# Order of the side work around a fused attention and MLP kernel: early differences, an earlier mean, and the weight differences one slot sooner

## The chip, the cores and the metric

The kernel runs on one core of a Trainium2 chip. The time is device microseconds of one execution, from runs on the chip; the median of the runs is given. A profiled execution gives, beside its time, when each instruction of each engine ran.

## The reference

Eight batches of eight heads, 576 tokens, head size 64; model width 512, hidden width 2048.

```python
scores = 1/sqrt(64) * q @ k.T                      # per batch and head
thresh = max(scores, -1) - tau
scores = where(scores >= thresh, scores, -1e9)
attn = exp(scores - max(scores, -1))
attn = attn / (sum(attn, -1) + 1e-09)
x = (attn @ v), heads side by side                 # (8, 576, 512)
mu, var = mean(x, -1), mean((x - mu)**2, -1)
xn = (x - mu) / sqrt(var + 1e-06) * g_ln
out = x + maximum(xn @ w_ch1, 0) @ w_ch2
```

w_ch1 is 512x2048 and w_ch2 2048x512. All products are done in float32.

## The kernel before, in words

**Slots.** The attention goes through 72 slots, nine for each batch. A slot takes 256 queries of each head of a pair (the fifth slot of a batch takes the last 64 queries of all heads). In a slot TensorE makes the scores (L394); VectorE reduces them to the negative maximum (L408); GpSimd makes the thresholds (L412); ScalarE takes the exponentials (L418); VectorE masks and sums them (L426) and takes the reciprocal (L431); GpSimd divides in four instructions (L442); VectorE transposes in blocks (L508); a DMA writes the result to a scratch tensor and another fetches it in the next slot (`fetch`, L519), and TensorE multiplies by v (L554), which ScalarE copies into `x` (L571). In slots whose successor needs a new pair of heads, `turn` (L331) scales q on GpSimd (L342) and transposes q and k on VectorE (L345 to L355).

**Groups.** The MLP goes through 16 groups of 288 tokens, two per batch. For each, GpSimd adds up x over its four pieces (`sum`, L586), TensorE turns that into a mean over all partitions (`mean_of`, L595, L601), ScalarE copies it out (L603), and VectorE subtracts it (`centre`, L606, L613: xc). `first_part` (L757) makes the hidden layer, and `second_quarters` (L903), or `second_plain` (L887) for group 0, makes the result.

**Seven products.** From group 1 on, six of the sixteen hidden tiles of the first part, and the whole second part, are done as a block product of two by two blocks with seven quarter products instead of eight. That needs sums and differences of blocks of both factors. Those of the tokens are made for each group: `xt3`, `xt2`, `xt4` on GpSimd (L752, L749, L752, in `quarters`, L835) and `xt1` on VectorE (L752). Those of the weights are made once, by the generator `differences` (L703): for w_ch1 (L715 to L719) s3 and s4 on GpSimd, s1 (in place) and s2 on VectorE, for two halves; for w_ch2 the same in 16 steps, four of each kind (L732). s1 overwrites what s3 reads; s2 reads s1; s4 reads s2. It is advanced by `first_part` of group 1, three steps after each tile (L874).

**Order.** All engines follow an order written out by hand. The loop over slots (L1081) calls the attention's steps, and at four quarters of a slot `second_part` (L1028), which takes steps of the MLP's generators as the plan `owed` has room. The MLP's additions and subtractions are put into lists, `rush` and `drops`, by `later` (L735), and `drip` (L622) empties these at the end of a slot's quarter by what room an engine has. An entry may be urgent: `drip` runs everything up to the last urgent entry that is due. `root` (L671, three instructions on VectorE, L674 to L678, which make the reciprocal square root of the variance more exact) is put into `rush` as urgent, due two quarters later if the norm is issued in the last quarter of a slot (L783). `need` (L744) runs a list until an entry is done.

**PSUM.** The MLP's products, the mean and the variance share two banks (`ps_ff`). While `second_quarters` runs, `banks_taken` keeps the mean out of them; the mean of the next group waits in `waiting_mean` and is issued within the last segment (L982 to L987).

The steps that the change touches are `differences`, `quarters`, the loop over tiles in `first_part` (L874), `second_plain`, and L983.

Of the kernel before, what the change touches and what calls it, by code (L numbers as in the profile page):

```python
# [12 lines left out]
ALU = mybir.AluOpType  # L13
# [5 lines left out]
def kernel(  # L19
# [31 lines left out]
    nc = tc.nc  # L51
# [5 lines left out]
    NK = DM // 128  # L57
# [5 lines left out]
    SLOTS = 2 * HP + 1  # L63
# [5 lines left out]
    SETS = [(5, 6, 7)]  # L69
# [58 lines left out]
    def load_v(u):  # L128
# [18 lines left out]
        out=tau_sb, in_=bass.AP(tensor=tau.tensor, offset=tau.offset, ap=[[0, 128], [1, 1]])  # L147
# [5 lines left out]
    for t in [er_sb] + v_rest:  # L153
# [10 lines left out]
        out=scl_sb, in0=tau_sb, scalar1=0.0, scalar2=SCALE, op0=ALU.is_ge, op1=ALU.mult  # L164
    )
    nc.vector.tensor_scalar(
        out=low_sb, in0=tau_sb, scalar1=0.0, scalar2=BIG, op0=ALU.is_lt, op1=ALU.mult
    )
    nc.vector.scalar_tensor_tensor(
        out=low_sb, in0=tau_sb, scalar=-1.0, in1=low_sb, op0=ALU.mult, op1=ALU.subtract  # L170
# [449 lines left out]
    aside, stores, drops, rush = [], [], [], []  # L620
# [50 lines left out]
    def root(y, x, t):  # L671
# [14 lines left out]
    w1 = {  # L686
        (i, j, k): w1_sb[NK // 2 * j + k][:, HD * 128 * i : HD * 128 * (i + 1)]
        for i in range(2)
        for j in range(2)
        for k in range(NK // 2)  # L690
    }
    w1_more = [
        [[t[:, k] for k in range(NK // 2)] for t in (
            consts.tile([128, NK // 2, len(ms) * 128], F32, name=f"w1_{q}_{ms[0]}") for q in (2, 3, 4)
        )]
        for ms in SETS
    ]
    more = []

    def part_tile(name):  # L700
        return ffn.tile([128, PART], F32, tag="part", bufs=2, name=name)

    def differences():  # L703


        flat = conversion.stage.rearrange("p a b -> p (a b)")
        flat4 = e_room[1].rearrange("p a b -> p (a b)")
        size = HM * HD * 128
        for t in (flat[:, :size], flat[:, size : 2 * size], flat4[:, :size]):
            more.append(t.rearrange("p (m d c) -> p m d c", m=HM, d=HD))  # L710
        for ms, (s2, s3, s4) in zip(SETS, w1_more):
            of = lambda i, j, k: w1[i, j, k][:, ms[0] * 128 : (ms[-1] + 1) * 128]
            for k in range(NK // 2):
                s1 = of(1, 0, k)
                nc.gpsimd.tensor_tensor(out=s3[k], in0=of(0, 0, k), in1=s1, op=ALU.subtract)  # L715
                yield
                nc.vector.tensor_tensor(out=s1, in0=s1, in1=of(1, 1, k), op=ALU.add)
                nc.vector.tensor_tensor(out=s2[k], in0=s1, in1=of(0, 0, k), op=ALU.subtract)
                nc.gpsimd.tensor_tensor(out=s4[k], in0=of(0, 1, k), in1=s2[k], op=ALU.subtract)  # L719
                yield  # L720
        s2, s3, s4 = more
        s1 = w2[1, 0]
        for eng, out, a, b, op in (
            (nc.gpsimd, s3, w2[0, 0], w2[1, 0], ALU.subtract),
            (nc.vector, s1, w2[1, 0], w2[1, 1], ALU.add),
            (nc.vector, s2, s1, w2[0, 0], ALU.subtract),
            (nc.gpsimd, s4, w2[0, 1], s2, ALU.subtract),
        ):
            for m in range(HM):
                for d in range(0, HD, 4):  # L730
                    at = (slice(None), m, slice(d, d + 4))
                    eng.tensor_tensor(out=out[at], in0=a[at], in1=b[at], op=op)  # L732
                    yield

    def later(calls_of, done, *calls, urgent=None, age=0):  # L735
        for what, cost, fn, eng, *args in calls:

            def go(what=what, fn=fn, eng=eng, args=args):
                fn(eng, *args)
                done.add(what)  # L740

            calls_of.append((urgent, now + age, eng, cost, go))

    def need(calls, done, *what):  # L744
        while not done.issuperset(what):
            calls.pop(0)[-1]()

    def add(eng, out, a, b):
        eng.tensor_tensor(out=out, in0=a, in1=b, op=ALU.add)  # L749

    def less(eng, out, a, b):
        eng.tensor_tensor(out=out, in0=a, in1=b, op=ALU.subtract)  # L752
# [4 lines left out]
    def first_part(g, done):  # L757
# [3 lines left out]
        plain = g == 0  # L761
# [3 lines left out]
        sums_of = differences() if g == 1 else iter(())  # L765
# [24 lines left out]
        def tile_of(d):  # L790
            p1 = ps_ff.tile([128, TOK], F32, tag="ff", name="p1")
            for c in range(NK):
                product(
                    p1, lhsT=w1_sb[c][:, d * 128 : (d + 1) * 128], rhs=xc[:, c],
                    start=(c == 0), stop=(c == NK - 1),
                )
                if c < NK - 1:
                    yield 1, 1
            nc.scalar.activation(hidden[:, d], p1, func=AF.Relu)  # L799
            yield 2, 1  # L800

        pool, dve = nc.gpsimd, nc.vector
        half = NK // 2
        ms = SETS[0]
# [3 lines left out]
        b11, b12 = xc[:, :half, early], xc[:, :half, late]  # L808
        b21, b22 = xc[:, half:, early], xc[:, half:, late]
        t2, t3 = hidden[:, ND - 3 : ND - 1, early], hidden[:, ND - 3 : ND - 1, late]  # L810
        t4, t1 = hidden[:, ND - 1].rearrange("p (c t) -> p c t", c=half), t3
        s2, s3, s4 = w1_more[0]
# [20 lines left out]
            yield 2, 0.5  # L833

        def quarters():  # L835
            later(
                rush, done, ("xt3", 1, less, pool, t3, b22, b12), ("xt2", 1, add, pool, t2, b11, t3),
                ("xt4", 1, less, pool, t4, b21, t2), urgent=pool,
            )
            yield quarter(1, old(0, 0), b11, h11)  # L840
            yield quarter(2, old(0, 1), b21)
            need(rush, done, "xt4")
            yield quarter(7, s3, t3)
            later(rush, done, ("xt1", 1, less, dve, t1, b12, b11), urgent=dve)
            yield quarter(6, s2, t2, h12)
            later(
                rush, done, ("xu2", 1, add, dve, h12, h12, h11), ("xu3", 1, add, dve, parts[7], parts[7], h12),
                ("x11", 1, add, pool, h11, h11, parts[2]), ("r11", 1, positive, pool, h11),
            )
            need(rush, done, "xt1")  # L850
            yield quarter(4, old(1, 1), t4, h21)
            later(rush, done, ("x21", 1, add, dve, h21, h21, parts[7]), ("r21", 1, positive, dve, h21))
            need(rush, done, "x11")
            yield quarter(3, s4, b22)
            later(rush, done, ("x12", 1, add, dve, h12, h12, parts[3]))
            yield quarter(5, old(1, 0), t1, h22)
            later(
                rush, done, ("xu4", 1, add, dve, h12, h12, h22), ("r12", 1, positive, dve, h12),
                ("x22", 1, add, dve, h22, h22, parts[7]), ("r22", 1, positive, dve, h22),
                urgent=dve,  # L860
            )
# [4 lines left out]
        for d in singles:  # L866
            while conversion.ended < 4 * (d // 4 + 1):
                yield 0, 0
            if d == low:
                yield from norm(True)  # L870
            if d == low + 2:
                need(rush, done, "root")
            yield from tile_of(d)
            for _ in range(1 if plain else 3):  # L874
                next(sums_of, None)
            ended += 1
            yield from norm()
            if not plain and d > 1:
                yield from next(between, ())
                yield from norm()  # L880
# [5 lines left out]

    def second_plain(g, rb, done):  # L887
        y = ffn.tile([128, NK, TOK], F32, tag="sq", bufs=1, name="y")
        for m in range(NK):
            p2 = ps_ff.tile([128, TOK], F32, tag="ff", name="p2")  # L890
            for d in range(ND):
                while conversion.ended <= conversion.n1 + 4 * m + d // 4:
                    yield 0, 0
                product(
                    p2, lhsT=w2_sb[:, m, d], rhs=hidden[:, d],
                    start=(d == 0), stop=(d == ND - 1),
                )
                if d < ND - 1:
                    yield 2, 1
            aside.append(lambda m=m, p2=p2: add_to_x(g, m, y[:, m], p2, rb))  # L900
            yield 2, 1

    def second_quarters(g, rb, done):  # L903

# [3 lines left out]
        s2, s3, s4 = more  # L908
        b11, b12 = hidden[:, :HD, early], hidden[:, :HD, late]
        b21, b22 = hidden[:, HD:, early], hidden[:, HD:, late]  # L910
# [39 lines left out]
        dve, pool = nc.vector, nc.gpsimd  # L950
# [29 lines left out]
        )  # L980
        yield 2, 0.5
        last = segment(s4, b22)  # L982
        for _ in range(12):  # L983
            yield next(last)
        banks_taken[0] = False
        while waiting_mean:
# [14 lines left out]
    QUARTERS = 4  # L1001
# [65 lines left out]
    else:  # L1067
# [3 lines left out]
        for i in range(ND):  # L1071
            nc.sync.dma_start(
                out=w2_sb[:, :, i],
# [123 lines left out]
```

## Time and profile before

| | |
|---|---|
| time, median of 3 runs | 1409.44 us (1409.41 to 1409.78) |
| the profiled execution: its own time | 1409.68 us |
| its span, first to last instruction | 1407.8 us |
| TensorE clock granted, mean | 0.991 |
| busy: TensorE, VectorE, GpSimd, ScalarE | 1327.4, 1024.6, 721.5, 497.2 us |
| TensorE busy, 0 to 190 us | 152.2 us |
| TensorE busy, 190 to 260 us (group 1's first part) | 59.84 us |
| TensorE busy, 260 to 1320 us | 1040.76 us |
| TensorE busy, 1320 to 1408 us | 74.55 us |
| slots 10, 11, 12 begin (scores on TensorE) | 193.03, 213.70, 234.18 us |

In the profile PE is TensorE, PEld its loading of weights, DVE VectorE, ACT ScalarE, POOL GpSimd and SP the engine that issues DMAs. A line number is that of the kernel's text. In a line of the order of time the columns are start and duration in us, engine, line, operation, the tile written and those read, shape and count of records; in brackets stands how long the engine was idle before, and whose instruction ended that. A matmul instruction shows as two records. L104 is a helper through which all products but the scores and the values go, so the tiles' names tell them apart: `p` is a tile of the first part, `quarter` and `seg` are quarter products of the first and the second part, `sc` scores or values. L749 and L752 are the helpers for additions and subtractions.

### The profile page before, as it was taken

The page shows a single profiled execution, that of the slowest core. Times are in us where ns is not written, and L with a number is a line of the kernel's source. Part 1 is how long each engine was busy: PE and PEld are TensorE (multiplying, and loading weights), DVE is VectorE, ACT ScalarE, POOL GpSimd, SP SyncE. Part 2 cuts the span into 40 slices and gives each one's busy share as a digit, 9 for nine tenths or more (in the row PEclk, how much of TensorE's full clock was granted, in tenths as well). Part 3 has the DMA queues.
Part 4 walks back from the last instruction along what each step waited for, and adds up shares of the span by engine and source line. Part 5 has one row for each costly group of instructions (what it writes and reads, how often), then busy time and mean ns, then how long its engine had stood idle before and what let it go on. Part 6 is the DMA issues. An engine that isn't in the chain of part 4 may idle for free. (4 is left out here: it accounts for less than half of the span.)

```text
span 1407.8 us, 38072 instructions
## 1 busy us (share of the span) xinstructions
PE 1327.4 (94%) x16128; PEld 1040.7 (74%) x16128; DVE 1024.6 (73%) x1680; ACT 497.2 (35%) x985; POOL 721.5 (51%) x887
## 2 busy tenths in 40 slices
PE   4878998999999999999999999999999999999996
PEld 3655665767878687876879677786978677786876
DVE  5997868767777788867777788767887777777331
ACT  3877623233232323323242323333242323323120
POOL 2444447554465555555455555555554544645433
PEclk8999999999999999999999999999999999999998
DMA  9612345346754466445755376455755376444211
GB/s 231 171 61 84 90 114 169 127 145 180 195 159 145 151 176 178 139 171 140 205 164 170 109 195 174 133 170 147 195 165 170 102 190 182 145 145 144 77 18 18
DMA packets 316393, 205.64 MB, mean 146 GB/s; under 512 B 242368, under 2 KB 273856, under 8 KB 308160
## 3 DMA queue, kind: packets, MB, share of 16 engines
q1 hardware_dynamic: 311456, 202.62, 50.2%
q8 instruction: 127, 2.08, 0.6%
q10 hardware_dynamic: 4736, 0.59, 0.4%
q14 instruction: 42, 0.34, 0.1%
q0 software_dynamic: 32, 0.00, 0.0%
HBM read 119.41 MB, written 83.76 MB: 144 GB/s over the span
## 5 line engine op out<-in xcount | busy, mean ns | idle before, releaser
L104 PE MATMUL p<-xc,w 128*64 128x288 f32 x2656 | 352.1, 409 | 24.0 <-ACT hidden L799 16.3
L408 DVE TENSOR_REDUCE neg<-sc 128x2 f32<-128x1152 f32 x144 | 188.5, 1350 | 196.2 <-PE sc L394 196.2
L104 PEld LDWEIGHTS p<-xc,w 128*64 128x64 f32 x2656 | 188.5, 137 | 144.0 <-ACT hidden L799 20.9
L418 ACT ACTIVATE e<-sc,neg 128x576 f32<-128x576 f32 x288 | 196.9, 743 | 254.9 <-DVE neg L408 243.7
L442 POOL TENSOR_SCALAR e<-e,den 128x576 f32<-128x576 f32 x252 | 206.7, 831 | 115.8 <-DVE den L431 115.6
L104 PE MATMUL seg<-hidden,w 128*64 128x144 f32 x3840 | 247.3, 286 | 1.4 <-DVE hidden L920 1.4
L104 PEld LDWEIGHTS seg<-hidden,w 128*64 128x64 f32 x3840 | 235.0, 137 | 11.9 <-issue 7.6
L426 DVE SCALAR_TENSOR_TENSOR e<-sc,thr,e 128x576 f32<-128x576 f32 x288 | 222.4, 813 | 15.7 <-ACT e L418 12.1
L412 POOL TENSOR_SCALAR thr<-neg,low_sb 128x2 f32<-128x2 f32 x144 | 43.8, 305 | 256.3 <-DVE neg L408 253.4
L394 PE MATMUL sc<-kT,qT 64*128 64x384 f32 (+3 forms) x1024 | 150.1, 424 | 20.0 <-DVE e L426 10.0
L508 DVE STREAM_TRANSPOSE et<-e 128x1152 f32<-128x1152 f32 x112 | 151.6, 1366 | 16.2 <-POOL e L442 15.8
L394 PEld LDWEIGHTS sc<-kT,qT 64*128 64x128 f32 x1024 | 94.1, 190 | 67.6 <-issue 16.2
L554 PE MATMUL sc<-em,v_in 128*64 128x256 f32 (+1 forms) x1408 | 131.1, 329 | 3.7 <-DVE e L426 3.2
L104 PE MATMUL seg<-hidden,stage 128*64 128x144 f32 x1920 | 123.4, 287 | 0.0
L104 PEld LDWEIGHTS seg<-hidden,stage 128*64 128x64 f32 x1920 | 117.5, 137 | 5.5 <-issue 4.0
L799 ACT ACTIVATE hidden<-p 128x288 f32<-128x288 f32 x166 | 68.3, 413 | 147.7 <-PE p L104 147.2
L920 POOL TENSOR_TENSOR hidden<-hidden 128x576 f32<-128x576 f32 x60 | 89.1, 1494 | 42.1 <-DVE hidden L755 26.1
L554 PEld LDWEIGHTS sc<-em,v_in 128*64 128x64 f32 x1408 | 86.7, 137 | 31.1 <-DVE e L426 3.7
L104 PEld LDWEIGHTS quarter<-hidden,w 128*64 128x64 f32 x1440 | 88.7, 137 | 22.9 <-ACT part L832 7.2
L104 PE MATMUL quarter<-hidden,w 128*64 128x144 f32 x1440 | 101.6, 288 | 3.8 <-ACT part L832 3.7
L571 ACT COPY x<-sc 128x256 f32<-128x256 f32 x60 | 22.3, 372 | 155.9 <-PE sc L554 149.9
L104 PEld LDWEIGHTS quarter<-xc,w 128*64 128x64 f32 x1080 | 67.5, 137 | 13.4 <-ACT hidden L799 4.3
(175 smaller groups left out, 1647.2 us busy)
## 6 DMA issues: line engine op xcount, KB each, us to landing
scr<-et SPq DMA_DIRECT2D x63, 1152.0 KB, 4.5
em<-scr SPq DMA_DIRECT2D x63, 1024.0 KB, 5.9
out_dram<-x SPq DMA_DIRECT2D x256, 36.0 KB, 4.3
q_in<-in_q_dram SPq DMA_DIRECT2D x124, 72.0 KB, 3.1
k_in<-in_k_dram SPq DMA_DIRECT2D x120, 72.0 KB, 3.0
er<-scr SPq DMA_DIRECT2D x63, 128.0 KB, 6.0
v_in<-in_v_dram SPq DMA_DIRECT2D x28, 256.0 KB, 4.4
w<-in_moe_w_ch_dram SPq DMA_DIRECT2D x10, 512.0 KB, 6.4
```

What stands on the lines that cost most here:

```text
L104: nc.tensor.matmul(out[r], lhsT=lhsT[:, r], rhs=rhs, **flags)
L394: nc.tensor.matmul(sc[h][64 * i : 64 * i + 64 if s == HP else 128, at : at + n], lhsT=ql[r] if s == HP else qT[r, half, j * 128 : (j + 1) ...
L408: nc.vector.tensor_reduce(out=neg[:, i], in_=pairs[h], axis=AXL.X, op=ALU.max, negate=True,)
L412: nc.gpsimd.tensor_scalar(out=thr[:, i], in0=neg[:, i], scalar1=-1.0, scalar2=low_sb, op0=ALU.mult, op1=ALU.add,)
L418: nc.scalar.activation(es[:, i], blocks[i], func=AF.Exp, bias=neg[:, i : i + 1])
L426: nc.vector.scalar_tensor_tensor(out=es[:, i], in0=blocks[i], scalar=thr[:, i : i + 1], in1=es[:, i], op0=ALU.is_ge, op1=ALU.mult, accum_o ...
L442: nc.gpsimd.tensor_scalar(out=es[:, i], in0=es[:, i], scalar1=den[:, i : i + 1], scalar2=1.0, op0=ALU.mult, op1=ALU.mult,)
L508: nc.vector.transpose(et[:, :, 64 * h : 64 * h + 64].rearrange("p n (j c) -> p j n c", j=2), es[:, 2 * h : 2 * h + 2].rearrange("p j (n c) ...
L554: nc.tensor.matmul(dst[64 * h : 64 * h + 64], lhsT=vt[:, h, c, :] if c < J else vr[:, h, :], rhs=pick(em[:, :, c] if c < J else er, hp, h) ...
L571: nc.scalar.copy(x_of(g)[:, hp, :QH], pv)
L799: nc.scalar.activation(hidden[:, d], p1, func=AF.Relu)
L920: eng.tensor_tensor(out=out[at], in0=in0[at], in1=in1[at], op=op)
```

## The change

Four edits:

- In `quarters` the three differences on GpSimd are issued at once, when the generator is first advanced (after the third tile), instead of by way of the list `rush`.
- In `second_quarters` the mean is issued after 8 instead of 12 steps of the last segment (16 instead of 24 instructions).
- The steps for w_ch1 become a generator of their own, `differences_1`, with a pause after each instruction. `second_plain` advances it at every second tile from slot 10 on, and runs out what is left at its end.
- The rest of `differences` (w_ch2) is advanced two steps after each tile of group 1, instead of three.

```diff
+    def differences_1():
         for ms, (s2, s3, s4) in zip(SETS, w1_more):
             of = lambda i, j, k: w1[i, j, k][:, ms[0] * 128 : (ms[-1] + 1) * 128]
             for k in range(NK // 2):
                 s1 = of(1, 0, k)
                 nc.gpsimd.tensor_tensor(out=s3[k], in0=of(0, 0, k), in1=s1, op=ALU.subtract)
                 yield
                 nc.vector.tensor_tensor(out=s1, in0=s1, in1=of(1, 1, k), op=ALU.add)
+                yield
                 nc.vector.tensor_tensor(out=s2[k], in0=s1, in1=of(0, 0, k), op=ALU.subtract)
+                yield
                 nc.gpsimd.tensor_tensor(out=s4[k], in0=of(0, 1, k), in1=s2[k], op=ALU.subtract)
                 yield
...
         def quarters():
-            later(
-                rush, done, ("xt3", 1, less, pool, t3, b22, b12), ("xt2", 1, add, pool, t2, b11, t3),
-                ("xt4", 1, less, pool, t4, b21, t2), urgent=pool,
-            )
+            less(pool, t3, b22, b12)
+            add(pool, t2, b11, t3)
+            less(pool, t4, b21, t2)
             yield quarter(1, old(0, 0), b11, h11)
             yield quarter(2, old(0, 1), b21)
-            need(rush, done, "xt4")
             yield quarter(7, s3, t3)
...
-            for _ in range(1 if plain else 3):
+            for _ in range(2):
                 next(sums_of, None)
...
     def second_plain(g, rb, done):
         y = ffn.tile([128, NK, TOK], F32, tag="sq", bufs=1, name="y")
+        sums_of = differences_1()
...
+                if now >= QUARTERS * (SLOTS + 1) and d % 2:
+                    next(sums_of, None)
                 if d < ND - 1:
                     yield 2, 1
...
+        for _ in sums_of:
+            pass
...
         last = segment(s4, b22)
-        for _ in range(12):
+        for _ in range(8):
             yield next(last)
```

More of the change, by code (lines that the diff above doesn't have):

```diff
@@ L701, in part_tile @@
         return ffn.tile([128, PART], F32, tag="part", bufs=2, name=name)
[L703 to L710, printed above, removed]
+    def differences_1():
         for ms, (s2, s3, s4) in zip(SETS, w1_more):
@@ L717, in differences @@
                 nc.vector.tensor_tensor(out=s1, in0=s1, in1=of(1, 1, k), op=ALU.add)
+                yield
                 nc.vector.tensor_tensor(out=s2[k], in0=s1, in1=of(0, 0, k), op=ALU.subtract)
+                yield
                 nc.gpsimd.tensor_tensor(out=s4[k], in0=of(0, 1, k), in1=s2[k], op=ALU.subtract)
                 yield
+    def differences():
+        flat = conversion.stage.rearrange("p a b -> p (a b)")
+        flat4 = e_room[1].rearrange("p a b -> p (a b)")
+        size = HM * HD * 128
+        for t in (flat[:, :size], flat[:, size : 2 * size], flat4[:, :size]):
+            more.append(t.rearrange("p (m d c) -> p m d c", m=HM, d=HD))
         s2, s3, s4 = more
```

## The prediction

> **What bounds the kernel now.** I read the engines' busy table first, then TensorE's waits in two stretches, then the order of time around each wait, then the order of instructions of both programs on each engine.
>
> ```profile
> PE 1327.4 (94%) x16128; PEld 1040.7 (74%) x16128; DVE 1024.6 (73%) x1680; ACT 497.2 (35%) x985; POOL 721.5 (51%) x887
> ```
>
> TensorE (PE) is the bound. In the steady stretch from 260 to 1320 us it is busy 1040.76 of 1060 us, so an edit gains only what PE idles, and costs what it makes PE idle. PE's waits there, then those from 190 to 260 us, where group 1 starts (in total, times, longest):
>
> ```profile
> PE p L104 <- ACT hidden L799: 10.2, 7, 1.6
> PE p L104 <- DVE xc L613: 2.8, 7, 0.4
> ```
>
> ```profile
> PE sc L554 <- DVE e L426: 3.2, 1, 3.2
> PE p L104 <- DVE xc L613: 2.5, 2, 2.2
> PE p L104 <- ACT hidden L799: 2.4, 1, 2.4
> PE quarter L104 <- ACT part L832: 2.0, 1, 2.0
> ```
>
> Seven times 10.2/7: one stall in each even group from 2 to 14. Group 4's, in order of time (start, duration, idle before in brackets; PE counts two records per instruction):
>
> ```profile
> 467.64 2.21 PE L394 MATMUL sc<-kT,qT 64*128 64x384 f32 x16
> ...
> 467.67 1.43 DVE L674 SCALAR_TENSOR_TENSOR hidden<-rb 128x288 f32<-128x288 f32 x1 [3.28 <-POOL y L944]
> ...
> 471.93 2.61 DVE L408 TENSOR_REDUCE neg<-sc 128x2 f32<-128x1152 f32 x2
> ...
> 473.31 1.37 ACT L418 ACTIVATE e<-sc,neg 128x576 f32<-128x576 f32 x2 [5.04 <-DVE neg L408]
> ...
> 475.04 2.16 PE L104 MATMUL p<-xc,w 128*64 128x288 f32 x16 [1.62 <-ACT hidden L799]
> ```
>
> The reduction (L408) could start 2.31 us after the scores (a free one: scores 486.11, reduction 488.42), at 469.95. The root's three instructions (L674 to L678, 467.67 to 471.04) and one addition of y (to 472.0) stand ahead of it. ACT's exponentials follow it, the RELU that frees the PSUM bank stands behind them, and PE waits 1.62.
>
> An odd group (3) has no PE wait, but no room either:
>
> ```profile
> 389.45 3.38 POOL L442 TENSOR_SCALAR e<-e,den 128x576 f32<-128x576 f32 x4
> ...
> 391.42 2.82 DVE L508 STREAM_TRANSPOSE et<-e 128x1152 f32<-128x1152 f32 x2 [1.28 <-POOL e L442]
> ...
> 394.16 0.63 DVE L674 SCALAR_TENSOR_TENSOR hidden<-rb 128x288 f32<-128x288 f32 x1
> ...
> 395.80 1.55 DVE L678 SCALAR_TENSOR_TENSOR rb<-hidden,rb 128x288 f32<-128x288 f32 x1
> ...
> 398.02 2.62 DVE L408 TENSOR_REDUCE neg<-sc 128x2 f32<-128x1152 f32 x2 [0.67 <-PE sc L394]
> ...
> 400.73 0.52 ACT L832 COPY part<-quarter 128x432 f32<-128x432 f32 x1
> ...
> 401.39 1.69 PE L104 MATMUL quarter<-hidden,w 128*64 128x144 f32 x24
> ```
>
> The copy that frees the bank ends at 401.25, and PE takes it at 401.39 without idling. The root ends 0.67 us before the reduction starts: that is all the slack.
>
> [...] L674 takes 0.46 us while POOL is idle (1349.74) and 1.43 us beside POOL's addition of 467.37 to 468.78; L678 at 395.80 ends 0.32 after POOL's 1.61 us multiplication (395.42 to 397.03). I use that rule below: end of POOL's instruction + 0.32. [...]
>
> **The change part by part.**
>
> *Even groups, root.* Giving the three differences (L752, L749, L752) at once takes their urgent entries out of the `rush` list; an urgent entry pulled all before it, the root too. By the order of instructions the root moves on VectorE behind the next slot's L426/L431 in all seven even groups; POOL's order stays there. The reduction then starts at 469.95, 1.98 earlier; L799 at 472.59, and PE finds a bank 0.47 later (474.57 to 475.04 before) at 473.06. It wants it at 475.04 − 1.62 = 473.42. The whole stall goes: 10.2 us in seven groups. What is late next: the root now stands ahead of L508, beside the divisions. With L426 from 472.8, the reciprocal ends at 476.3, the root by the rule at 478.3, L508 at 480.9 (481.2 before). The next fetch is issued at 486.56 and lands 5.9 us later (page, part 6) at 492.5, for products at 499.23; hidden.
>
> *Even groups, mean.* Eight instructions of about 0.13 us (3.11 us for 48 records) go behind it: 1.0 us earlier. Of the 0.41 us that PE waits for xc, VectorE idles 0.34 for the mean's copy; before that it is busy with L431. So 0.34 in groups 4 to 14; nothing in group 2, where L613 follows L431 at once. 6 × 0.34 = 2.0 us. In the odd groups only four instructions move and PE waits for nothing there. In the last group L613 stands behind L657's transposes, ended at 1337.74, which wait for POOL's addition: nothing of its 1.64 us.
>
> *Odd groups, POOL.* In groups 3 to 13 (six) the differences move ahead of the four divisions. They took 2.65 us (392.80 to 395.45). In group 3 they now start at 389.45 and end near 392.1; the divisions (0.73 each) end in pairs at 393.6 and 395.1; L508's second half follows, to 396.5 instead of 394.24. The root, queued behind it, meets POOL's long multiplication (395.15 to 396.56), long addition (to 398.15) and short multiplication (to 399.1): its three end at 396.88, 398.47 and 399.42. The reduction starts at 399.36 instead of 398.02, so 1.34 late; the exponentials and L832 are queued behind, and PE waits 1.34 − 0.09 (PE was ready 0.09 after it could have had the bank) = 1.25. Six times: 7.5 us. [...] A root that never meets POOL takes 1.35 and ends at 397.8: 0 us. [...]
>
> *Group 1.* In slot 10 seven of the eight steps of w_ch1 go ahead of L426 (the last L719 follows the divisions) instead of behind the centring. VectorE's second L717 must wait for POOL's second L715, which is queued behind L719, which needs VectorE's first L718. Worked with L715/L719 1.0 us and L717/L718 0.56: thresholds to 198.32, L715 to 199.32, L717 to 199.92, the turns of k and q and one of x to 201.86, L718 to 202.36, L719 and L715 to 204.47, L717 and L718 to 205.66, then L426 at 205.6 instead of 200.27. Queued behind: L651 and the centring L613, for which PE waits already 2.19 at 204.86. PE starts 5.3 later. Its bounds: 4.5 if POOL's steps take 0.8 beside an idle VectorE, 6 if L717 waits for q_in's POOL instruction (0.74).
> What comes back, in times less 5.3 (so PE's old times are the measure). POOL's first four steps of w_ch2 (2.5 per pair) and L773 (three, 2.6) now run from 207.8 to 215.6, before slot 11's thresholds; behind these stand only the three differences (2.6), then q_in: it ends at 222.4 instead of 225.2. VectorE turns q (0.9), does two steps of w_ch2 (1.2) and starts L426 at 224.5 instead of 227.82; its second one ends at 226.1, and PE, which wants its bank at 226.28, doesn't wait the 3.15 of 229.43. Then VectorE has to 227.8 for L426, 1.5 for two steps, to 231.9 for L508 (last division 229.75), 1.3 for the root (POOL idle), 1.3 for two steps and 0.4 for L752: slot 12's reduction starts at 234.7. The old 239.22 less the 3.15 would be 236.07, so the PE wait of 2.42 shrinks by 1.4. POOL in slot 12 has, from the reduction on, the thresholds (2.9), a pair of w_ch2 (2.5), the divisions (3.6), the last pair (2.5, which stood before the thresholds till now) and L749 (1.1), which frees the part tile for L832: 12.8 with the gaps, instead of 10.1 (239.22 to 249.34). PE's 2.0 there becomes 4.7. Sum 5.3 − 3.15 − 1.4 + 2.7 = +3.5; the returns are good to 2 us and more, so 0 to +6.
>
> *Queues.* SP's order is the same; its fetches follow VectorE by as much as that moves. Nothing else is added or removed.
>
> Sum: −10.2 − 2.0 + 7.5 + 3.5 = −1.2. The profiled execution took 1409.68 (span 1407.8, 1.9 around it), 0.24 above the median 1409.44. From the median: 1408.2. About 0.2%, 2.8 us, can be told from no change, so this is a forecast of no measurable difference made of four large terms.
>
> **Rivals.**
> 1. *The odd groups stay whole.* If the root slips between POOL's instructions, −12.2 + 3.5 = −8.7: 1400.7. For it: uncontended, 1.35 us fit. Against: POOL's queue after the divisions is without a gap for 4 us in the trace. Half the stall gives −5 (1404.5). A group 1 that gains (POOL less late than worked out) has the same sign.
> 2. [...] Place: root behind L508 in groups 3 to 13; price six times the delay. Decides from (2.8 + 8.7)/6 = 1.9 us a group; at 2.2 it is +4.5: 1413.9. For it: L678 already took 1.55. Against: the count above.
> 3. *The even stall doesn't go*, as another entry stands ahead of L408: +9, 1418.4. Against: VectorE's order in all seven groups has only y's addition there, whose inputs are ready 5 us before.
>
> **Chances.** Forecast 0.47, rival 1 with its halves 0.28, rival 2 0.21, rival 3 0.04. So faster 0.28, same 0.47, slower 0.25. The range, 1401.5 to 1414, reaches nearly to both middle rivals.
>
> **What would show it.** PE's wait for L799 in even groups gone, L408 2.31 after the scores; xc waits 0.1. In odd groups L508 ends about 2.2 later, L408 starts about 1.3 later and a new PE wait for L832 of 1.25 stands in six groups. In slot 10 L426 starts near 205.6 and PE waits 7.5 for xc; no wait for L426 in slot 11; near 4.7 for L832 in slot 12. I am wrong if L408 in the odd groups is on time, or if the centring of group 1 isn't 5 us later.

## The result, and the profile after

| | before | after |
|---|---|---|
| median, runs on one chip | 1409.61 us (1409.41 to 1410.53) | 1408.35 us (1408.2 to 1410.87) |
| ratio, from all runs, with 95% interval | | 0.9994 [0.9977, 1.0011] |
| profiled execution, span | 1409.68, 1407.8 us | 1408.34, 1406.5 us |

The forecast was 1408.2 us and no measurable difference; so it came out. The total is right, but all four of its terms are too small, two gains and two losses, and these errors cancel. That is what the rest shows.

TensorE's busy time hardly differs:

```profile
PE 1326.8 (94%) x16128; PEld 1043.7 (74%) x16128; DVE 1013.2 (72%) x1680; ACT 497.6 (35%) x985; POOL 725.2 (52%) x887
```

TensorE's waits from 264 to 1320 us (total, times, longest). The wait for hidden is gone, that for xc is 0.4 instead of 2.8, and one for the part tile is new: six of 1.30 us in the odd groups. The other six, of 0.33, were there before (one of them as 0.15).

```profile
PE quarter L104 <- ACT part L838: 9.8, 12, 1.3
...
PE p L104 <- DVE xc L613: 0.4, 1, 0.4
```

From 190 to 264 us, group 1's start. Two short waits have become long ones, and two have become shorter:

```profile
PE p L104 <- DVE xc L613: 7.8, 1, 7.8
PE quarter L104 <- ACT part L838: 4.8, 1, 4.8
PE p L104 <- ACT hidden L805: 1.1, 1, 1.1
PE sc L554 <- DVE e L426: 0.6, 1, 0.6
```

Group 4 in order of time (start, duration). The reduction starts 2.31 us after the scores, the product that waited 1.62 us follows without a wait, and the root stands behind the masking, beside the divisions:

```profile
474.31 2.21 PE L394 MATMUL sc<-kT,qT 64*128 64x384 f32 x16
...
476.62 2.62 DVE L408 TENSOR_REDUCE neg<-sc 128x2 f32<-128x1152 f32 x2 [4.58 <-PE sc L394]
...
478.45 1.64 PE L104 MATMUL quarter<-xc,w 128*64 128x144 f32 x24
...
479.92 2.11 PE L104 MATMUL p<-xc,w 128*64 128x288 f32 x16
...
482.85 0.44 DVE L674 SCALAR_TENSOR_TENSOR hidden<-rb 128x288 f32<-128x288 f32 x1
```

Group 3, where the divisions now follow the differences. The second half of the transposes ends at 402.67, the root runs into GpSimd's additions and multiplications and ends at 405.57, and the reduction starts 3.70 us after the scores instead of 2.31. ScalarE's copy is queued behind, and TensorE waits 1.29:

```profile
398.35 2.90 POOL L442 TENSOR_SCALAR e<-e,den 128x576 f32<-128x576 f32 x4
...
399.85 2.82 DVE L508 STREAM_TRANSPOSE et<-e 128x1152 f32<-128x1152 f32 x2 [3.03 <-POOL e L442]
...
401.79 2.21 PE L394 MATMUL sc<-kT,qT 64*128 64x384 f32 x16
...
402.71 1.57 POOL L755 TENSOR_TENSOR y<-y,x 128x576 f32<-128x576 f32 x1
403.04 1.55 DVE L677 TENSOR_TENSOR hidden<-hidden 128x288 f32<-128x288 f32 x1
...
404.24 1.01 POOL L953 TENSOR_TENSOR y<-y,rb 128x288 f32<-128x288 f32 x1
404.63 0.94 DVE L678 SCALAR_TENSOR_TENSOR rb<-hidden,rb 128x288 f32<-128x288 f32 x1
...
405.49 2.61 DVE L408 TENSOR_REDUCE neg<-sc 128x2 f32<-128x1152 f32 x2
...
408.19 0.52 ACT L838 COPY part<-quarter 128x432 f32<-128x432 f32 x1
...
408.85 1.69 PE L104 MATMUL quarter<-hidden,w 128*64 128x144 f32 x24 [1.29 <-ACT part L838]
```

**Where the time went, slot by slot.** Waits add up what the profile sees of idle time. A second count needs no ends of matmuls: the begin of each slot's scores (first L394) in the trace after, less the same before. How much this shift grows in a stretch is what that stretch lost or gained.

| stretch | forecast | measured by the slots |
|---|---|---|
| up to slot 10, ahead of any edit | 0 | −0.66 |
| group 1 (slots 10 to 15) | +3.5 | +7.34 |
| even groups, root: group 2, then 4 to 14 | −10.2 | −0.61 − 6 x 1.87 = −11.8 |
| even groups, mean: 4 to 14 | −2.0 | −6 x 0.79 = −4.7 |
| odd groups 3 to 13 | +7.5 | +6 x 1.39 = +8.3 |
| sum | −1.2 | −1.5 (the last slot's shift is −1.32; small shifts such as +0.13 at slot 37 make the rest) |

The first row, which no edit explains, is a difference between the two executions. The traces of the experiments below, whose order is the same up to slot 10, lie between −0.87 and +1.31 there.

Slot by slot, group 1's +7.34 is +6.78 in slot 10, −2.65 in slot 11, +3.03 in slot 12, 0 in slot 13 and +0.18 in slot 14, where TensorE waits for a fetch. That last wait is between 1.2 and 1.9 us from trace to trace.

### The profile page after: what moved, and what is told of

The parts are those of the page before. It is cut to its first block, busy times and chain, and to the rows that moved or that the text cites. A ratio compares the mean times of both kernels' runs of the same rounds, so it can differ in the third digit from the quotient of the medians.

```text
span 1406.5 us, 38066 instructions
## 1 busy us (share of the span) xinstructions
PE 1326.8 (94%) x16128; PEld 1043.7 (74%) x16128; DVE 1013.2 (72%) x1680; ACT 497.6 (35%) x985; POOL 725.2 (52%) x887
## 5 line engine op out<-in xcount | busy, mean ns | idle before, releaser
L426 DVE SCALAR_TENSOR_TENSOR e<-sc,thr,e 128x576 f32<-128x576 f32 x288 | 222.4, 811 | 12.8 <-ACT e L418 12.1
L394 PE MATMUL sc<-kT,qT 64*128 64x192 f32 (+3 forms) x1024 | 149.1, 424 | 19.6 <-DVE qT L354 10.0
L394 PEld LDWEIGHTS sc<-kT,qT 64*128 64x128 f32 x1024 | 93.7, 190 | 66.9 <-issue 16.9
L554 PE MATMUL sc<-em,v_in 128*64 128x256 f32 (+1 forms) x1408 | 132.4, 331 | 2.5 <-DMA em<-scr 1.9
L554 PEld LDWEIGHTS sc<-em,v_in 128*64 128x64 f32 x1408 | 87.8, 138 | 31.4 <-DMA em<-scr 2.1
```

The lines of the kernel that those rows point to most:

```text
L394: nc.tensor.matmul(sc[h][64 * i : 64 * i + 64 if s == HP else 128, at : at + n], lhsT=ql[r] if s == HP else qT[r, half, j * 128 : (j + 1) ...
L426: nc.vector.scalar_tensor_tensor(out=es[:, i], in0=blocks[i], scalar=thr[:, i : i + 1], in1=es[:, i], op0=ALU.is_ge, op1=ALU.mult, accum_o ...
L554: nc.tensor.matmul(dst[64 * h : 64 * h + 64], lhsT=vt[:, h, c, :] if c < J else vr[:, h, :], rhs=pick(em[:, :, c] if c < J else er, hp, h) ...
```

## Experiments

My theory after the comparison: the effects are separate and add up as in the table; the odd groups lose because VectorE's root runs beside GpSimd's long multiplication and addition (L677 takes 1.55 us there in group 3, and 0.46 at 1348.90, where GpSimd is idle); and of group 1's 7.3 us a part isn't waiting but a halved TensorE clock (the share of the clock that the trace says was granted, 0.50 instead of 1.00). The rivals are named with each run. All times are medians, beside runs of the kernel before on the same chip.

**The early differences alone.** In `quarters` only:

```diff
-            later(
-                rush, done, ("xt3", 1, less, pool, t3, b22, b12), ("xt2", 1, add, pool, t2, b11, t3),
-                ("xt4", 1, less, pool, t4, b21, t2), urgent=pool,
-            )
+            less(pool, t3, b22, b12)
+            add(pool, t2, b11, t3)
+            less(pool, t4, b21, t2)
...
-            need(rush, done, "xt4")
```

> The kernel before with the three early differences alone; mean and weight differences as before. My theory, after the slot times of the changed kernel: every even group from 4 to 14 starts 1.87 us sooner (its root no longer ahead of the reduction, the 1.6 us wait for hidden gone), every odd group from 3 to 13 loses 1.39 us (a wait of 1.3 us for the part tile), group 2 gains 0.6. Sum 6 x (1.39 - 1.87) - 0.6 = -3.5: about 1406.0 us. Rival (the prediction's own sizes, 1.46 gained and 1.25 lost): -10.2 + 7.5 = -2.7, about 1406.8. Rival 2: the two edits depend on each other and the early differences alone lose the even gain: 1414 or more, with the hidden waits still in the trace.

Measured: 1405.71 beside 1409.59 us, ratio 0.9974 [0.9966, 0.9982]. The slots give −1.85 to −1.87 in each even group from 4 on, −0.61 in group 2, and +1.37 to +1.40 in each odd group. The theory's 1406.0 holds; the prediction's own sizes (1406.8) are not excluded by the median, but they are by the slots. The wait for xc is still 2.9 us here, so it belongs to the mean.

**The mean alone.**

```diff
-        for _ in range(12):
+        for _ in range(8):
             yield next(last)
```

> The kernel before with the mean after 8 steps instead of 12 and nothing else. From the shift of the scores in the changed kernel: 0.79 us for each of groups 4 to 14, so 4.7 us less than before, 1404.8. From the prediction's working (only VectorE's idle 0.34 comes back): 2.0 less, 1407.5. Rival (the stall behind the exponentials takes it back): 1409.5.

Measured: 1404.39 beside 1409.39 us, 0.9967 [0.9955, 0.9978]; the slots give −0.78 to −0.80 six times. The theory holds, and the prediction's 2.0 us for this edit is outside the interval (0.9978 is −3.1 us). Why 0.79 and not 0.34 is read from the traces of the two main kernels. Group 4 before, then in the changed kernel:

```profile
455.97 1.95 POOL L442 TENSOR_SCALAR e<-e,den 128x576 f32<-128x576 f32 x2 [0.20 <-DVE den L431]
456.22 2.37 DVE L613 TENSOR_TENSOR xc<-x,sum 128x288 f32<-128x288 f32 x4 [0.34 <-ACT sum L603]
...
457.07 5.30 PE L104 MATMUL p<-xc,w 128*64 128x288 f32 x40 [0.41 <-DVE xc L613]
```

```profile
463.26 2.01 DVE L613 TENSOR_TENSOR xc<-x,sum 128x288 f32<-128x288 f32 x4
463.44 2.37 POOL L442 TENSOR_SCALAR e<-e,den 128x576 f32<-128x576 f32 x2 [0.20 <-DVE den L431]
463.95 5.10 PE L104 MATMUL p<-xc,w 128*64 128x288 f32 x40
```

The whole wait of 0.41 goes. The row of products is 0.2 shorter, since it had also been held up in small pieces (the largest 0.18) for the later parts of xc; the centring takes 2.01 instead of 2.37 us, and VectorE now starts 0.18 us before GpSimd's division and not 0.25 us after it. That leaves 0.79 − 0.41 − 0.2 = 0.18 us, which the profile hides: it counts idle time from the modelled end of the matmul before. The root's stall shows the same, with this line of before and those of group 4 above:

```profile
471.77 1.64 PE L104 MATMUL quarter<-xc,w 128*64 128x144 f32 x24
```

Before, 3.27 us lay from the begin of the 24 quarter records to that of the next products (471.77 to 475.04); after, 1.47 (478.45 to 479.92), though the quarter row is put at 1.64. So 1.80 us was lost where the page says 1.62: without a wait the next row begins some 0.17 us before the end that the profile gives the row ahead.

**All but the weight differences.** The early differences and the mean, with `differences` as before.

> Early differences and earlier mean as in the changed kernel, weight differences as in the kernel before. Theory: the changed kernel's order of the weight differences costs 7.3 us around group 1 (scores of slot 14 shift from -0.66 at slot 10 to +6.68 at slot 15), of which 2.7 by a halved TensorE clock after the two long waits. So 1408.35 - 7.3, about 1401.0, no stretch at half clock between 200 and 300 us, and the odd groups' wait of 1.3 still there. Rival (the even groups' gain and the odd groups' loss are themselves different once group 1 is undone, or group 1's cost comes from the early differences): 1405 or more.

Measured: 1401.5 beside 1409.39 us, 0.9944 [0.993, 0.9959]. The time holds. One part of the expectation fell: the clock does halve here (granted 0.50), for 6.8 us, after the wait of 3.12 us in slot 11, though in the trace of before a wait of 3.15 there left it at 1.00. And this half clock costs almost nothing in the end: slot 11 is 2.79 us longer than before, but slot 12 is 2.47 shorter, as TensorE, now late itself, no longer waits the 2.42 us for hidden. The last section comes back to this clock.

**The weight differences alone.** `differences_1` from slot 10 on and two steps a tile, the rest as before.

> The kernel before with the two edits for the weight differences alone (w_ch1 from slot 10 on, two steps a tile for the rest). From the slot times: group 1 loses 7.3 us, all else as before: 1409.5 + 7.3 = 1416.8 us, with the waits of 7.8 and 4.8 us and two stretches of half clock. Rival (the prediction's own size for group 1, +3.5): 1413.0.

Measured: 1417.12 beside 1409.75 us, 1.0058 [1.0043, 1.0073]. The theory holds and +3.5 (1413.0) is outside the interval; only the wait for xc is 7.2 us here and not 7.8. The three parts of the change, each alone, give −3.9, −5.0 and +7.4 us: together −1.5, where the whole change measured −1.26. Each of these medians is uncertain by 1 to 2 us. The slots say it more closely: some 1.87 for the root and 0.79 for the mean in an even group, alone as in the whole change, and from slot 10 to slot 15 +7.1 alone and +7.3 in the whole. So the parts don't depend on each other.

**Is it the clock in group 1?** The waits there changed by +5.6 (7.8 instead of 2.2, for xc), −2.6, −1.3 and +2.8: +4.5, but the slots say 7.3. The stretches after the two long waits show why. First the row of products in slot 10 before, up to the products with v:

```profile
204.86 1.91 PE L104 MATMUL p<-xc,w 128*64 128x288 f32 x12 [2.19 <-DVE xc L613]
207.03 3.13 PE L104 MATMUL p<-xc,w 128*64 128x288 f32 x24 [0.27 <-DVE xc L613]
209.99 1.90 PE L554 MATMUL sc<-em,v_in 128*64 128x256 f32 x16
```

Of the kernel after, two stretches of 3.41 us (width, TensorE busy with records, weight loads, VectorE, ScalarE, GpSimd, granted TensorE clock, share of DMA, GB/s):

```profile
209.79:213.20 3.41, 3.41 (x14) 1.71 (x16) 3.41 (x5) 0.00 (x0) 3.41 (x4) 0.50 0.02 5
254.92:258.33 3.41, 3.41 (x20) 2.19 (x22) 0.00 (x0) 0.26 (x1) 1.16 (x1) 0.54 0.34 137
```

A clock of 0.50, and 14 records in 3.41 us where full speed has some 27 (40 in 5.10). In the trace of before it is 1.00 in all of group 1. By the trace's record of the clock it is halved from 206.86 to 213.68 and from 254.64 to 258.06: TensorE worked 3.9 and 3.1 us at half speed. Half of each is lost, an estimated 1.95 and 1.57 us. In slot 10 some of this comes back, since before the row also waited for the later parts of xc: from its begin to the products with v it took 5.13 us (204.86 to 209.99) and takes 6.32 now (209.79 to 216.11), 1.19 more. The clock's price is thus 1.19 + 1.57 = 2.8 us, what is left of 7.3 beside the waits. To test it, the wait was filled with products whose result is overwritten:

```diff
+            if g == 1 and d == singles[0]:
+                for _ in range(14):
+                    product(p1[:, :256], lhsT=avg_sb, rhs=w2_sb[:, 3, 14:16], start=True, stop=True)
             for c in range(NK):
                 product(
                     p1, lhsT=w1_sb[c][:, d * 128 : (d + 1) * 128], rhs=xc[:, c],
```

> The changed kernel with 14 further products (avg_sb by 256 columns of w_ch2, thrown away: the real product of the same tile overwrites them) ahead of group 1's first product, about 6.4 us of work in TensorE's 7.8 us wait for xc. Clock theory: without the long idle time the clock stays at full speed, the half clock stretch of 6.8 us near 206 to 213 us is gone, slot 11 begins 1.2 us sooner, and of it what the waits of slots 11 and 12 don't take up remains: 1407.2 us. Rival: the half clock doesn't come from the idle time: the stretch stays, slot 11 begins within 0.2 us of the changed kernel's, 1408.4. Rival 2: the clock stays up, but VectorE's and GpSimd's work in slots 11 and 12 sets the end of group 1: slot 11 sooner, slot 13 not, 1408.4.

The same two stretches, of the kernel with the filled wait:

```profile
209.79:213.20 3.41, 1.95 (x14) 0.73 (x14) 3.41 (x6) 0.00 (x0) 3.33 (x4) 1.00 0.00 0
254.92:258.33 3.41, 3.41 (x18) 2.19 (x20) 0.00 (x0) 0.26 (x1) 1.16 (x1) 0.50 0.32 132
```

The half clock in slot 10 is gone (granted 1.00 instead of 0.50), though the work there is more, and the row takes 5.14 us again instead of 6.32. So it was the idle time that halved the clock here, and the half clock cost 1.18 us there, as expected (1.2). Slot 10 is in all 1.72 us shorter than in the changed kernel; the other 0.54 isn't the clock's, but comes from a race between two instructions that the edit doesn't touch. The changed kernel, then the one with the filled wait:

```profile
198.63 0.75 POOL L342 TENSOR_SCALAR q_in<-q_in,scl_sb 128x576 f32<-128x576 f32 x1
198.68 1.10 DVE L712 TENSOR_TENSOR w<-w,w 128x384 f32<-128x384 f32 x1 [1.38 <-POOL w L710]
```

```profile
200.35 1.13 POOL L342 TENSOR_SCALAR q_in<-q_in,scl_sb 128x576 f32<-128x576 f32 x1
200.40 0.56 DVE L712 TENSOR_TENSOR w<-w,w 128x384 f32<-128x384 f32 x1 [1.37 <-POOL w L710]
```

The two begin 0.05 us apart, and one of them takes longer: VectorE's 1.10 instead of 0.56 us in the changed kernel, GpSimd's 1.13 instead of 0.75 in the other, where all that follows comes 0.5 us sooner. The wait for xc is 7.8 us in the changed kernel and in the one with the late root, and 7.2 in two other traces with this order; that the same race makes this difference is my estimate from the 0.5 us.

In slot 12, where the wait of 4.8 us was left as it is, the half clock lasted longer this time, to 260.1 us, and slot 12 lost 1.02 us more. Over slots 10 to 15 the kernel with the filled wait gains 1.4 us on the changed one: 1.72 less 1.02, and 0.7 from the fetch of slot 14, which varies by as much without any edit. The time, 1407.81 beside 1409.75 us (0.9986 [0.9977, 0.9994]), can't tell this from the changed kernel. So the first rival is refuted by the clock in slot 10. The second is refuted too: slots 11 and 12 begin 1.7 us sooner, counted from slot 10, and yet TensorE idles no longer in them (0.7 and 5.9 us in both kernels). What slot 12 loses is the clock's own: 5.2 us of its work fall into half clock instead of 3.1. What no run here shows is a gain in time from keeping the clock up all through group 1.

**Is it the turns of VectorE and GpSimd in slot 10?** The steps of w_ch1 in pairs of one kind (s3, s3, s1, s1, s2, s2, s4, s4), on the changed kernel.

> The changed kernel with the steps of w_ch1 in another order, s3 s3, s1 s1, s2 s2, s4 s4 for each half, so that VectorE and GpSimd don't wait for each other by turns. If the turns are what delays the masking of slot 10 (start 205.2 us), it starts near 203, the wait for xc shrinks from 7.8 to about 5.3 us, and the time is about 2.5 us less, 1405.9; TensorE still falls to half clock after it. Rival: the steps' own durations set it, and nothing changes: within 0.7 us of 1408.4.

Measured: 1407.67 beside 1409.59 us, 0.9986 [0.998, 0.9993]. From slot 10's begin to the masking it takes 11.0 instead of 12.8 us, and the wait is 6.0 instead of 7.8; 2.5 was expected, and q_in, now behind two of GpSimd's s3, is one reason (VectorE idles 2.37 us for it). Of the 1.8 us some 0.5 may be the race in which VectorE's instruction took 1.10 us in the changed kernel; the order avoids it here. But slot 11 begins only 0.9 us sooner, counted from slot 10. The other half goes to the clock. TensorE's first row after the wait, in the changed kernel and then in this one:

```profile
209.79 6.49 PE L104 MATMUL p<-xc,w 128*64 128x288 f32 x36 [7.79 <-DVE xc L613]
```

```profile
208.56 7.38 PE L104 MATMUL p<-xc,w 128*64 128x288 f32 x36 [5.99 <-DVE xc L613]
```

The same 36 records take 0.89 us longer. The clock's stretch is no shorter for the shorter wait (6.8 us both times), so 5.7 us of the work fall into it (to 214.24 us) instead of 3.9: half of the difference is the 0.89. The expectation was too high by what the clock takes, and by q_in; the turns, with the race, cost about 1.8 us of the 5.6 by which the wait grew. The time alone doesn't tell this kernel from the changed one.

**What delays the root of the odd groups?** The changed kernel with GpSimd's long multiplication and addition of y left out of groups 2 to 12, the even ones, which run beside the odd groups' root. The lower half of their result isn't finished by this kernel.

```diff
+            if j is None and g % 2 == 0 and 2 <= g <= 12:
+                later(
+                    drops, done, *((f"o{m}", 1, store, dve, g, m, y[:, m]) for m in ends), age=2
+                )
+                return
             z, x = y[at], groups[g][at]
```

> The changed kernel, but GpSimd's long multiplication and long addition of the lower half of y are left out in groups 2 to 12, the even ones: this part of the output is not computed. They are what GpSimd runs beside the root of the odd groups. [...] the root then meets only the short multiplication and addition, its three instructions take 0.44 + 0.5 + 0.5 and a little, the reduction of slots 22, 31, ... begins at most 0.3 us late, and the six waits of 1.30 us for the part tile fall below 0.4: about 1408.4 - 6 x 1.1 = 1401.8 us. Rival: it is the late transposes (second L508) that delay the reduction, whatever GpSimd does beside the root: the waits stay at 1.0 to 1.3 and the time at 1407 to 1408.4.

Measured: 1403.27 beside 1409.59 us, 0.9949 [0.9932, 0.9965]. Its waits for the part tile, and its group 3:

```profile
PE quarter L104 <- ACT part L838: 4.0, 12, 0.3
```

```profile
401.00 2.82 DVE L508 STREAM_TRANSPOSE et<-e 128x1152 f32<-128x1152 f32 x2 [3.04 <-POOL e L442]
...
403.74 0.62 DVE L674 SCALAR_TENSOR_TENSOR hidden<-rb 128x288 f32<-128x288 f32 x1
404.39 0.87 DVE L677 TENSOR_TENSOR hidden<-hidden 128x288 f32<-128x288 f32 x1
405.29 0.46 DVE L678 SCALAR_TENSOR_TENSOR rb<-hidden,rb 128x288 f32<-128x288 f32 x1
405.67 2.62 DVE L408 TENSOR_REDUCE neg<-sc 128x2 f32<-128x1152 f32 x2
```

The transposes are as late as in the changed kernel. The root's middle instruction takes 0.87 instead of 1.55 us, the last 0.46 instead of 0.94, and the reduction starts 2.75 us after the scores (402.92) instead of 3.70. The slots give 0.94 to 0.97 us back in each odd group. So of the 1.39 us some 0.96 come with GpSimd's two long instructions, and 0.44 are the late transposes with the root that still stands behind them (2.75 − 2.31). Both theories have a share; that of GpSimd's work is the larger. The time fell by about 5 us where 6.6 were expected, for that reason.

**The root behind the reduction in the odd groups too.** On the changed kernel:

```diff
-                    urgent=nc.vector, age=2 if part > 2 else 0,
+                    urgent=nc.vector, age=2,
```

> The changed kernel, with the root of every group due two quarters later, so that in odd groups too it stands behind the next slot's L431 and not ahead of L408. Theory (the root behind the late transposes holds up the reduction): the wait of 1.3 before the quarter product in groups 3 to 13 goes, six times 1.39 = 8.3 us less: 1400.0. Rival (the late divisions reach TensorE by the transposes and the fetch, or by the exponentials): the waits stay and the time is within 1 us of 1408.3.

Measured: 1399.57 beside 1409.39 us, 0.993 [0.9913, 0.9946]. Its group 3, and its waits for the part tile, of which only short ones are left:

```profile
402.16 2.21 PE L394 MATMUL sc<-kT,qT 64*128 64x384 f32 x16
```

```profile
403.11 1.40 POOL L755 TENSOR_TENSOR y<-y,x 128x576 f32<-128x576 f32 x1
...
404.48 2.62 DVE L408 TENSOR_REDUCE neg<-sc 128x2 f32<-128x1152 f32 x2 [1.41 <-PE sc L394]
```

```profile
PE quarter L104 <- ACT part L838: 1.7, 5, 0.3
```

VectorE idles 1.41 us until the scores are there and starts 2.32 after their begin. Nothing new is late for it.

**The version that beats both.** Early differences, earlier mean and the root behind the reduction everywhere, without the edits of the weight differences.

> Early differences, earlier mean, the late root of the second experiment, and the weight differences as before. If the parts add up: 1409.5 - 16.5 (even groups) = 1393.0, no wait over 0.5 in groups 3 to 14. If the odd groups' loss only moves elsewhere: 1401.

Measured: 1394.12 us (1392.38 to 1395.29) beside 1409.39, 0.9891 [0.9876, 0.9905]. In every group from 2 on the long waits are gone. What is left at group 1's start are three of the four waits of the kernel before, 3.2, 2.5 and 2.0 us.

**A slower pace of the weight differences.** The same kernel with two steps after each tile instead of three.

> Early differences, earlier mean, root late in both kinds of groups and the weight differences as before (1394.1 us), but advanced two steps after each tile instead of three. If the pace alone makes GpSimd late in slot 11, the wait of 3.15 us for the masking there and the half clock after it go, and the time is 3 to 5 us less: 1389 to 1391. Rival: the same steps then stand in the slots behind and the waits only move: 1393 to 1395.

Measured: 1395.8 us, 0.9902 [0.9887, 0.9917]: no gain, as the rival has it (1393 to 1395). Slot 11 is 2.2 us shorter, and its 16 records of L554 take 1.95 us, as in the trace of before, where the clock is 1.00 there. But the wait of 2.0 us in slot 12 becomes 3.2, and the 16 records behind it take 3.06 us, which I read as the half clock; slots 12 and 13 lose 2.3 and 1.6 us. The work only moves, and by the slots group 1 is 1.5 us longer than with three steps.

## Why the prediction came out, step by step

*What bounds, and the sum's form: right.* TensorE's busy time is the same, and every gain or loss is idle time of TensorE at a place that the prediction named, besides the clock.

*Even groups, root: mechanism right, size short.* Reduction 2.31 after the scores, stall gone, root beside the divisions, nothing else late. −10.2 was the sum of the waits; −11.8 was lost in truth, since the profile counts idle time from modelled ends (1.62 for 1.80) and the row after the wait takes some 0.05 us more (2.16 us at 475.04, 2.11 at 479.92). The even spread, "seven times 10.2/7", wasn't so either: group 2's wait was 0.38 us, the other six 1.62 to 1.65. Each of the seven slots gained 0.23 us more than its wait.

*Even groups, mean: the step that failed by the most in proportion.* "0.34 in groups 4 to 14" took VectorE's idle time for the gain. TensorE's row is what counts: 0.41 of wait, 0.2 of small waits within the row, 0.18 that isn't seen: 0.79. The prediction was right that group 2 gets nothing.

*Odd groups: right.* Forecast were the root's ends at 396.88, 398.47 and 399.42, the reduction at 399.36 and a wait of 1.25. Less the 6.08 us by which this slot begins later, the root's ends come at 396.93, 398.51 and 399.49 and the reduction at 399.41; the wait is 1.30 in all six groups, and the slots say 1.39. The measure by which the root was worked out, 0.32 us after GpSimd's instruction, holds: L677 ends at 404.59, 0.31 after GpSimd's addition (404.28), and L678 at 405.57, 0.32 after its multiplication (405.25). Removing GpSimd's work takes two thirds of the loss away (0.94 to 0.97 of 1.39 us), so this is shown and not only fitted. The first rival (odd groups whole) and the second (1.9 us a group) are out.

*Group 1: waits right, the sum not.* L426 of slot 10 was put at 205.6 and came at 205.17, or 205.83 counted from slot 10; the wait for xc at 7.5 and was 7.8, or 7.2 in two other traces, which the prediction's bounds ("if L717 waits for q_in's POOL instruction") had in them; the one for L426 was to vanish and left 0.6; 2.42 was to shrink by 1.4 and did by 1.3; 4.7 was 4.8. Four waits, +4.5 in all instead of +3.5. What failed is that the term counted nothing but waits: after each of the two long ones TensorE ran at half clock (granted 0.50), 2.8 us more. With that the +7.3 lies outside the term's own bounds of 0 to +6. Ahead of each fall to 0.50 the trace holds 3.41 us without a matmul, from 203.44 and from 251.23 us. The trace of before has a case too: TensorE waits 2.77 us up to 112.25, and from 112.14 to 115.55 us the granted clock is 0.50. Waits of 7.5 and 4.7 us stood in the prediction; this stretch should have been held beside them.

*The total.* Measured less forecast is −4.37 in the even groups, +0.84 in the odd ones, +3.84 in group 1 and −0.66 at the start: −0.35 in all. The errors of the even groups and of group 1 are each larger than the 2.8 us that could be told from no change; that the forecast of "no measurable difference" held is luck in the sum, though not in the signs, which were right four times out of four.

## What to carry to other kernels

An edit that does several things is to be tried in parts: here two of the three were worth 8 us together and the third cost nearly all of it, and one more line (the root later) made it 15 us. A wait of TensorE is worth more than the profile's idle time: here 0.1 to 0.2 us more for most, and 1.2 and an estimated 1.6 us more for the two that halved the clock. But count the slots behind as well: where TensorE would have waited there anyway, as in the kernel without the weight differences, the loss comes back. If VectorE work like this root is on the path, look at what GpSimd runs at that moment, and move it to where GpSimd isn't, or behind what TensorE waits for: L677 and L678 took 0.46 us each with GpSimd idle, and 1.55 and 0.94 beside it in group 3.

## What the runs showed of the hardware that was not expected

The clock's half-speed stretches around group 1 last 3.41 us (254.64 to 258.06 in the changed kernel) or 6.83 (206.86 to 213.68 there; about 6.8 in four other traces). What they cost at first is half of the time that TensorE works in them, not a fixed price: an estimated 1.95 us in slot 10 with 3.9 us of work, 0.9 more when a shorter wait put 5.7 us of work into the stretch. In the traces of the two main kernels all changes of the clock within the span lie on a grid of 3.41 us: in the changed kernel the falls at 111.28, 206.86 and 254.64 are 28 and 14 steps apart. The grid lies elsewhere against the kernel in the two: the first of these falls comes 0.50 us ahead of TensorE's restart after a wait of 2.77 us (111.78), and in the trace of before 0.11 us ahead of the same restart (112.14 and 112.25).

A stretch of 3.41 us without a matmul isn't needed for the fall. This is seen at the wait in slot 11, which is 3.12 to 3.15 us long in five traces. It halved the clock in the kernel without the weight edits and in the best version, and left it up before and with the early differences or the mean alone. The step of the grid in which most of the wait lies, in the first two and then in two of the others (columns as above; the clock is still 1.00 in it):

```profile
226.01:229.42 3.41, 1.35 (x15) 0.70 (x10) 3.14 (x7) 0.67 (x2) 0.23 (x1) 1.00 1.11 319
226.38:229.79 3.41, 1.21 (x12) 0.56 (x8) 3.25 (x7) 0.53 (x2) 0.12 (x1) 1.00 1.12 313
224.78:228.19 3.41, 1.50 (x18) 0.85 (x13) 2.96 (x7) 0.82 (x2) 0.41 (x1) 1.00 1.13 304
224.12:227.53 3.41, 1.67 (x20) 1.02 (x16) 2.81 (x7) 0.96 (x2) 0.57 (x1) 1.00 1.03 324
```

In the first two TensorE is busy for 0.40 and 0.36 of the step, and the clock falls to 0.50 behind it; in the others for 0.44 and 0.49, and it stays up (1.00 before; with the early differences the next 16 records take 1.95 us, as they do before). The wait is the same, and its place on the grid differs. That this place, and with it the busy share, decides is my estimate from these four, which are too few to show it. In the same way the clock stayed low to 258.06 us in slot 12 of the changed kernel and to about 260.1 with the filled wait, after the same 4.8 us. No edit here sets that place, so one trace of a kernel doesn't tell what its other runs do: in the runs of the kernel before on record the mean granted clock lies between 0.988 and 0.995, and those with the lower clock tend to be the longer ones (correlation −0.67).
